# Attention and two feed-forward layers on one core: one block of the first product gathered in PSUM

## The chip, the cores and the metric

The kernel runs on one core of one Trainium2 chip. The metric is the device time of one execution in microseconds (us), from launch to the last store; lower is better. In the rows, PE is TensorE (the matmuls), PEld its weight loads, DVE is VectorE, ACT is ScalarE, POOL is GpSimd and SP is SyncE, which issues the transfers.

## The reference

An attention with local and strided masks is followed by two feed-forward layers on the same 2,304 tokens (model width 512, inner width 2,048), all in float32:

```python
x = attention(q, k, v)                  # 4 batches, 8 heads, 576 positions, width 64
h = x @ moe_w_in;   g = h * clip(h + 3, 0, 6) / 6
x = g @ moe_w_out
h = x @ moe2_w_in;  g = h * tanh(softplus(h))      # Mish
return g @ moe2_w_out
```

## The kernel before, in words

**Numbers and layout.** Activations lie transposed: `xs0` to `xs3` hold 128 of the 512 model columns each, with the tokens along the row. A matrix operand is split into a high and a low part, both of type fp32r, and a product is three matmuls (`mm3`, L1106 to L1108: low weights by high data, high by low, high by high). The weights of the input side are in tiles `win`, those of the output side in `wout`, the split data in `x` (5 slots) and `g`, `g_late` (9 slots).

**Two by two blocks in seven products.** Apart from the attention and a piece of the first layer (20 "plain" steps, until about 167 us), each feed-forward layer works on blocks: a unit is a range of 2 x 384 tokens and one or more slices `fp` of the inner width (names ending in 0 and 1 where a unit has two). In a unit the four blocks of the first product h (two halves of tokens by two halves of the slice, called a11, a12, a21, a22) come from seven block products in place of eight, after Winograd. Each of the seven is two `mm3` (q = 0, 1), so six matmuls of 128x384. `PRODUCTS` (L45) is the order of the seven, and `CHAIN` says which are added up in the same PSUM bank: bank a takes a11, s2, s1, s4 one after the other, bank b takes s3 and a22, bank c takes a12. There are 42 pairs of a unit and a slice that go this way, 18 in the first layer and 24 in the second.

**What happens between the products.** `first_evict` reads a bank when a product has been added to it, before the next product may add more. Three sums are snapped to SBUF tiles by a copy (`c` after a12, `v` after s3, `u` after s2); then DVE adds a later state of another bank onto the tile: c + a11 gives block a11, u + a22 gives a21, v + s1 gives a22. The fourth block stays in bank a until s4 has been added. `activated` then applies the activation: in the first layer a Relu6 on ACT and a product on DVE (L1238, L1240), in the second a Mish on ACT (L1247), which needs another table of functions than the attention and the first layer, so that one ACT_TABLE_LOAD stands ahead of the first Mish. The four activated blocks are summed and split into `g`, and a second set of seven products with `wout` adds up the layer's output in `xs`.

**Who sets the order.** No queue or scheduler of the compiler decides: `Plan` (L150 to L304) simulates the engines with costs, factors (`SLOW`), due times and small constants (`FIRST_PACE`, `SOON`, `OVERLAP`, `BIAS`, `GUARD_DVE`, ...), and emits the instructions of each engine in the order that comes out. Each engine takes its rows in that order. The plan also picks the PSUM bank: first products use banks 0 to 3, second products banks 4 to 7; an operation with `frees` gives a bank back. Operations without a fixed engine (`add(None, ...)`) go to whichever the plan finds done first. The plan knows nothing of the ACT_TABLE_LOAD. While PE works on the first products of one unit it also works on the second products of the unit before, in turns that the plan mixes.

In the attention (16 units of a batch and two heads, in among the plain steps) the sums of the softmax get a guard against zero (L735 on ACT or L737 on DVE; `GUARD_DVE` says for how many units DVE does it). POOL or DVE then multiplies the exponentials `e` (L741), which PE transposes (L750).

Of the kernel before, what the change touches and what calls it, by code (L numbers as in the profile page):

```python
# [41 lines left out]

BOTH = ((0, 0, 0), (0, 1, 1, 1))

PRODUCTS = ("a12", "a11", "s3", "s2", "a22", "s1", "s4")  # L45
SECOND = ("a11", "s3", "s2", "a22", "s1", "a12", "s4")
CHAIN = {"a11": "a", "s2": "a", "s1": "a", "s4": "a", "a12": "c", "s3": "b", "a22": "b"}
W_OF = {"a11": (0, 0), "a12": (0, 1), "s2": (2, 6), "s1": (2, 8), "s4": (1, 4), "s3": (3, 10), "a22": (3, 12)}
# [31 lines left out]


ORIGIN = 600
START, FIRST_PACE = 26026, 2749
UNIT = 113
MASKS_DUE = 18211

SOON = 57

HALF_ROWS = 1.8

SPLIT = 2
KEEP, SWITCH = 1413, 100
GUARD_DVE, AGAIN_POOL, ABS_DVE = 0, 4, 1
HALF_PACE = 4687
EARLY_W, EARLY_G, EARLY_X = 10496, 7917, 10732
OVERLAP = 15258
UNIT_Y, UNIT_X = 11126, 19146
LEAD = 0.1313


BIAS = {"act": -116, "dve": 455, "pool": 239}
FIRST_BIAS = {"act": -1424, "dve": 440, "pool": 9}
BIAS_FROM = 37262

SLOW = {"pe": 1.0, "act": 1.0405, "dve": 1.0525, "pool": 0.9269, "dma": 1.2861}

# [210 lines left out]
def copy_ns(n, psum=False):  # L319

    return {"act": act_ns(n, psum), "dve": dve_ns(n if psum else n / 2)}
# [17 lines left out]
def attention_then_two_ffns(ctx, tc, qkv, masks, wts, out):  # L339
# [20 lines left out]
    add = plan.add  # L360
# [9 lines left out]
    pool = ctx.enter_context(tc.tile_pool(name="main", bufs=1, side="right"))  # L370
# [70 lines left out]
    t = START  # L441
# [776 lines left out]
    def build(u):  # L1218
# [32 lines left out]
        def chain_of(keys, use, before, product, evict, first_due):  # L1251


            nonlocal due
            due = first_due
            banks_of = {(c, key): Bank(use) for c in "abc" for key in keys}
            last, gone = {}, {}
            for i, kind in enumerate(PRODUCTS if use == "h" else SECOND):
                c = CHAIN[kind]
                for key in keys:  # L1260
                    bank, started = banks_of[c, key], (c, key) in last
                    deps = [*last.get((c, key), []), *gone.get((c, key), [])]
                    if i == 0:
                        deps.extend(before)
                    prev = None
                    parts = product(i, kind, key)
                    for x, (more, emit) in enumerate(parts):
                        due += cost
                        prev = add(
                            "pe", cost, lambda emit=emit, bank=bank, first=not started and x == 0, last=x == len(parts) - 1: emit(banks[bank.n][:, :n], first, last),  # L1270
                            [prev, *deps, *more], due=due, bank=None if started or x else bank,
                        )
                        if not started and x == 0:
                            opened[use].append(prev)
                    last[c, key] = [prev]
                    gone[c, key] = evict(i, kind, key, prev, bank, lambda bank=bank: banks[bank.n][:, :n])

        x_now, snaps = {}, {}

        def first_product(i, kind, fp):  # L1280

# [17 lines left out]
        def first_evict(i, kind, fp, o, bank, psum):  # L1299

            x_now[kind][2].append(o)
            if u.closes:
                in_use[m, fp][W_OF[kind][0]].append(o)
            if kind in ("a12", "s3", "s2"):
                at = snaps[kind, fp] = take({"a12": "c", "s3": "v", "s2": "u"}[kind])
                o = add(None, copy_ns(n, True), lambda eng: copy(eng, at.tile(), psum()), [o, *at.old], frees=bank if kind == "a12" else None)
                at.ready = [o]
                return [o]
            if kind == "s4":
                activated(fp, "a12", psum, [o], take("t"), bank)  # L1310
                return []
            of, to = {"a11": ("a12", "a11"), "a22": ("s2", "a21"), "s1": ("s3", "a22")}[kind]
            at = snaps[of, fp]
            o = add(
                "dve", dve_ns(n), lambda: nc.vector.tensor_tensor(at.tile(), psum(), at.tile(), ALU.add),
# [236 lines left out]
```

## Time and profile before

| | before |
|---|---|
| runs, us | 821.84, 823.63, 823.14 (median 823.14) |
| the profiled execution's own time, us | 823.42 |
| its span, first to last instruction, us | 821.6 |
| mean granted TensorE clock | 0.996 |
| DVE busy, us (share) | 699.0 (85%) |
| ACT busy, us (share) | 440.9 (54%) |
| POOL busy, us (share) | 244.7 (30%) |

The page of a profile counts as busy the time in which an instruction of the engine runs; matmuls overlap, each 128x384 one is shown as 0.33 us long while the next starts 0.17 us after it. So for PE the distance between starts says more than the busy time. In the timeline "[0.36 <-PE bank L1108]" behind a row means that the engine stood idle for 0.36 us ahead of it and what ended that. "x2" is a run of like instructions drawn together. Rows name tiles without their numbers.

### The profile page before, as it was taken

To read this page: it belongs to the slowest core of one execution; us is meant where nothing else is said; L and a number is where in the kernel's file an instruction comes from. 1 tells how busy PE (TensorE), PEld (TensorE's weight loads), DVE (VectorE), ACT (ScalarE), POOL (GpSimd) and SP (SyncE) were. 2 spreads that over 40 slices of the span, in tenths; PEclk is the share of its full clock that TensorE was granted. 3 is DMA by queue.
4 is the path that set the end of the run, shared out by engine and by line. 5 is a ranking of instruction groups with operands and counts; after the bars stand their busy time and mean duration, and the time that the engine had idled before them with its cause. 6 is when DMAs were issued, how large, how long until landed. Compare 5 with 4: busy or idle time off the path is not lost.

```text
span 821.6 us, 17074 instructions
## 1 busy us (share of the span) xinstructions
PE 809.5 (99%) x6672; PEld 776.9 (95%) x6672; DVE 699.0 (85%) x1332; ACT 440.9 (54%) x936; POOL 244.7 (30%) x229
## 2 busy tenths in 40 slices
PE   8899999999999999999999999999999999999998
PEld 5678888899999999999999999999999999999998
DVE  5699977899999657997999999966999999998666
ACT  2576667676554434444446567545455554455442
POOL 3424321112322200111214223100556544564332
PEclk9899999999999999999999999999999999999999
DMA  7966671466678587865774545865767766765832
GB/s 224 245 190 212 208 224 40 167 249 254 247 284 321 192 291 235 270 247 201 265 254 187 226 165 240 280 215 190 262 226 243 242 214 234 251 213 189 256 116 106
DMA packets 49381, 182.32 MB, mean 222 GB/s; under 512 B 6292, under 2 KB 15636, under 8 KB 49300
## 3 DMA queue, kind: packets, MB, share of 16 engines
q1 hardware_dynamic: 49300, 181.23, 64.4%
q8 instruction: 52, 0.85, 0.4%
q14 instruction: 29, 0.24, 0.1%
HBM read 138.74 MB, written 42.47 MB: 221 GB/s over the span
## 4 chain that ended last, share of the span: by engine, by line
PE 95%; DMA 2%; SPq 1%; DVE 1%; issue 1%; ACT 0%; POOL 0%; ACTq 0%; POOLq 0%
PE bank L1106 30%; PE bank L1108 29%; PE bank L1107 29%; PE bank L796 2%; PE bank L644 2%; DMA xs<-in_qkv_dram 1%; PE bank L750 1%; SPq L533 1%; DMA y<-keep 0%; PE bank L752 0%; PE bank L701 0%; PE bank L1476 0%; ACT pt L365 0%; SPq L880 0%; DVE xs L1379 0%
## 5 line engine op out<-in xcount | busy, mean ns | idle before, releaser
L1106 PE MATMUL bank<-x,win 128*128 128x384 f32 (+3 forms) x668 | 228.1, 341 | 0.5 <-POOL win L857 0.5
L1107 PE MATMUL bank<-x,win 128*128 128x384 f32 (+3 forms) x668 | 226.2, 339 | 0.0
L1108 PE MATMUL bank<-x,win 128*128 128x384 f32 (+3 forms) x668 | 226.1, 338 | 0.0
L1106 PE MATMUL bank<-g,wout 128*128 128x384 f32 (+3 forms) x512 | 176.0, 344 | 0.2 <-DVE xs L1379 0.2
L1108 PE MATMUL bank<-g,wout 128*128 128x384 f32 (+3 forms) x512 | 174.0, 340 | 0.0
L1107 PE MATMUL bank<-g,wout 128*128 128x384 f32 (+3 forms) x512 | 173.9, 340 | 0.0
L1106 PEld LDWEIGHTS bank<-x,win 128*128 128x128 f32 x668 | 125.4, 188 | 4.2 <-POOL win L857 0.9
L1107 PEld LDWEIGHTS bank<-x,win 128*128 128x128 f32 x668 | 125.4, 188 | 2.4 <-DVE x L857 0.4
L1108 PEld LDWEIGHTS bank<-x,win 128*128 128x128 f32 x668 | 125.4, 188 | 2.2
L1389 DVE TENSOR_TENSOR xs<-bank,xs 128x384 f32<-128x384 f32 x174 | 95.3, 550 | 32.6 <-PE bank L1108 31.6
L1106 PEld LDWEIGHTS bank<-g,wout 128*128 128x128 f32 x512 | 96.1, 188 | 3.1 <-DVE xs L1379 0.8
L1108 PEld LDWEIGHTS bank<-g,wout 128*128 128x128 f32 x512 | 96.1, 188 | 2.3
L1107 PEld LDWEIGHTS bank<-g,wout 128*128 128x128 f32 x512 | 96.2, 188 | 1.7 <-issue 0.2
L1108 PE MATMUL bank<-g_late,wout 128*128 128x384 f32 x204 | 68.1, 334 | 0.0
L1106 PE MATMUL bank<-g_late,wout 128*128 128x384 f32 x204 | 68.1, 334 | 0.0
L1107 PE MATMUL bank<-g_late,wout 128*128 128x384 f32 x204 | 68.1, 334 | 0.0
L906 DVE SCALAR_TENSOR_TENSOR wa<-raw,wa 128x512 uint32<-128x512 uint32 x64 | 49.1, 769 | 0.4
L992 POOL TENSOR_TENSOR w<-w 128x256 f32<-128x256 f32 x21 | 17.7, 843 | 91.3 <-DVE w L923 87.4
L365 ACT CAST g<-t 128x384 fp32r<-128x384 f32 (+3 forms) x59 | 31.4, 536 | 19.9 <-DVE t L1167 6.8
L857 POOL TENSOR_TENSOR win<-w,win 128x512 fp32r<-128x512 f32 (+1 forms) x20 | 26.0, 1305 | 46.9 <-ACT win L365 35.0
L365 ACT CAST win<-w 128x512 fp32r<-128x512 f32 (+1 forms) x55 | 30.7, 570 | 16.4 <-DVE w L923 7.7
L365 ACT COPY v<-bank 128x384 f32<-128x384 f32 x42 | 20.1, 480 | 35.6 <-PE bank L1108 32.8
(151 smaller groups left out, 1469.5 us busy)
## 6 DMA issues: line engine op xcount, KB each, us to landing
x<-kept_s SPq DMA_DIRECT2D x60, 768.0 KB
x<-kept_a SPq DMA_DIRECT2D x45, 768.0 KB
raw<-in_wts_dram SPq DMA_DIRECT2D x64, 512.0 KB
kept_s<-x SPq DMA_DIRECT2D x24, 768.0 KB
kept_a<-x SPq DMA_DIRECT2D x18, 768.0 KB
qk<-in_qkv_dram SPq DMA_DIRECT2D x14, 576.0 KB
keep<-y SPq DMA_DIRECT2D x24, 192.0 KB
out_dram<-xs SPq DMA_DIRECT2D x24, 192.0 KB
```

Of the source, the lines that this page charges most:

```text
L365: nc.scalar.copy(out, src)
L533: return add("dma", 400, lambda: nc.sync.dma_start(to(rows), src), due=MASKS_DUE)
L644: nc.tensor.matmul(banks[both[h].n][g * QN:(g + 1) * QN, slot * WK:(slot + 1) * WK], src.q[h * D:(h + 1) * D, n // 6, n % 2 * QN:(n % 2 + ...
L750: nc.tensor.transpose(banks[turned[0].n][:, j * P:(j + 1) * P], e[:, t:t + 2].rearrange("p s k -> p (s k)"), ident)
L796: nc.tensor.matmul(o[h * D:(h + 1) * D], src.v[rows, NB + others(local).index(n) if n in others(local) else i, h * D:(h + 1) * D], pt[rows ...
L857: lambda eng: engines[eng].tensor_tensor(lo(), src(), hi().bitcast(F32), ALU.subtract),
L906: lambda: nc.vector.scalar_tensor_tensor(ai, high, 0xC0000000, ai, ALU.bitwise_and, ALU.bitwise_or),
L992: lambda eng: engines[eng].tensor_tensor(of[out], of[x], of[y], ALU.subtract), [*on[x], *on[y]], lock=("dve", "pool"),
L1106: nc.tensor.matmul(o, low_w, high, start=first, stop=False, skip_group_check=True)
L1107: nc.tensor.matmul(o, high_w, low, start=False, stop=False, skip_group_check=True)
L1108: nc.tensor.matmul(o, high_w, high, start=False, stop=last, skip_group_check=True)
L1389: "dve", dve_ns(n), lambda: nc.vector.tensor_tensor(y(), src(), y(), ALU.add), [prev, y_sums[key]], due=due, frees=frees,
```

## The change

a11 becomes the first product and a12 the second. When a11 is in bank a, it is copied from there into bank c (a copy from PSUM to PSUM) in place of a12's copy to the tile `c`. a12's matmuls then add onto that bank, so its first matmul no longer starts a new sum and has to come after the copy. The block a11 is complete in bank c after a12, the DVE add onto the tile `c` falls away, and the activation reads the bank and gives it back. s2 and s3 change places in the order of the products. The constants of the plan are new, all of them numbers that shift the order.

```diff
@@ -42,7 +42,7 @@
 
 BOTH = ((0, 0, 0), (0, 1, 1, 1))
 
-PRODUCTS = ("a12", "a11", "s3", "s2", "a22", "s1", "s4")
+PRODUCTS = ("a11", "a12", "s2", "s3", "a22", "s1", "s4")
 SECOND = ("a11", "s3", "s2", "a22", "s1", "a12", "s4")
 CHAIN = {"a11": "a", "s2": "a", "s1": "a", "s4": "a", "a12": "c", "s3": "b", "a22": "b"}
 W_OF = {"a11": (0, 0), "a12": (0, 1), "s2": (2, 6), "s1": (2, 8), "s4": (1, 4), "s3": (3, 10), "a22": (3, 12)}
@@ -80,29 +80,29 @@
 
 
 ORIGIN = 600
-START, FIRST_PACE = 26026, 2749
+START, FIRST_PACE = 26026, 2816
 UNIT = 113
 MASKS_DUE = 18211
 
-SOON = 57
+SOON = 63
 
 HALF_ROWS = 1.8
 
 SPLIT = 2
 KEEP, SWITCH = 1413, 100
-GUARD_DVE, AGAIN_POOL, ABS_DVE = 0, 4, 1
+GUARD_DVE, AGAIN_POOL, ABS_DVE = 2, 4, 1
 HALF_PACE = 4687
 EARLY_W, EARLY_G, EARLY_X = 10496, 7917, 10732
-OVERLAP = 15258
-UNIT_Y, UNIT_X = 11126, 19146
+OVERLAP = 20001
+UNIT_Y, UNIT_X = 11448, 19146
 LEAD = 0.1313
 
 
-BIAS = {"act": -116, "dve": 455, "pool": 239}
-FIRST_BIAS = {"act": -1424, "dve": 440, "pool": 9}
+BIAS = {"act": -55, "dve": 474, "pool": 239}
+FIRST_BIAS = {"act": -1424, "dve": 424, "pool": 9}
 BIAS_FROM = 37262
 
-SLOW = {"pe": 1.0, "act": 1.0405, "dve": 1.0525, "pool": 0.9269, "dma": 1.2861}
+SLOW = {"pe": 1.0, "act": 1.0417, "dve": 1.0525, "pool": 0.9235, "dma": 1.2861}
 
 
 
@@ -1255,11 +1255,16 @@
             due = first_due
             banks_of = {(c, key): Bank(use) for c in "abc" for key in keys}
             last, gone = {}, {}
+            if use == "h":
+                h_banks.update({key: banks_of["c", key] for key in keys})
             for i, kind in enumerate(PRODUCTS if use == "h" else SECOND):
                 c = CHAIN[kind]
                 for key in keys:
                     bank, started = banks_of[c, key], (c, key) in last
                     deps = [*last.get((c, key), []), *gone.get((c, key), [])]
+                    seeded = use == "h" and kind == "a12"
+                    if seeded:
+                        deps.extend(gone["a", key])
                     if i == 0:
                         deps.extend(before)
                     prev = None
@@ -1267,15 +1272,15 @@
                     for x, (more, emit) in enumerate(parts):
                         due += cost
                         prev = add(
-                            "pe", cost, lambda emit=emit, bank=bank, first=not started and x == 0, last=x == len(parts) - 1: emit(banks[bank.n][:, :n], first, last),
-                            [prev, *deps, *more], due=due, bank=None if started or x else bank,
+                            "pe", cost, lambda emit=emit, bank=bank, first=not started and not seeded and x == 0, last=x == len(parts) - 1: emit(banks[bank.n][:, :n], first, last),
+                            [prev, *deps, *more], due=due, bank=None if started or seeded or x else bank,
                         )
-                        if not started and x == 0:
+                        if not started and not seeded and x == 0:
                             opened[use].append(prev)
                     last[c, key] = [prev]
                     gone[c, key] = evict(i, kind, key, prev, bank, lambda bank=bank: banks[bank.n][:, :n])
 
-        x_now, snaps = {}, {}
+        x_now, snaps, h_banks = {}, {}, {}
 
         def first_product(i, kind, fp):
 
@@ -1301,15 +1306,20 @@
             x_now[kind][2].append(o)
             if u.closes:
                 in_use[m, fp][W_OF[kind][0]].append(o)
-            if kind in ("a12", "s3", "s2"):
-                at = snaps[kind, fp] = take({"a12": "c", "s3": "v", "s2": "u"}[kind])
-                o = add(None, copy_ns(n, True), lambda eng: copy(eng, at.tile(), psum()), [o, *at.old], frees=bank if kind == "a12" else None)
+            if kind == "a11":
+                to = h_banks[fp]
+                return [add(
+                    None, copy_ns(n, True), lambda eng: copy(eng, banks[to.n][:, :n], psum()), [o], bank=to,
+                )]
+            if kind in ("s3", "s2"):
+                at = snaps[kind, fp] = take({"s3": "v", "s2": "u"}[kind])
+                o = add(None, copy_ns(n, True), lambda eng: copy(eng, at.tile(), psum()), [o, *at.old])
                 at.ready = [o]
                 return [o]
-            if kind == "s4":
-                activated(fp, "a12", psum, [o], take("t"), bank)
+            if kind in ("s4", "a12"):
+                activated(fp, {"s4": "a12", "a12": "a11"}[kind], psum, [o], take({"s4": "t", "a12": "c"}[kind]), bank)
                 return []
-            of, to = {"a11": ("a12", "a11"), "a22": ("s2", "a21"), "s1": ("s3", "a22")}[kind]
+            of, to = {"a22": ("s2", "a21"), "s1": ("s3", "a22")}[kind]
             at = snaps[of, fp]
             o = add(
                 "dve", dve_ns(n), lambda: nc.vector.tensor_tensor(at.tile(), psum(), at.tile(), ALU.add),
```

How this moves rows shows best at three places. The first is ACT at the changeover from the first layer to the second; the names are those of the last section, x_73 is the split data, bank3_64 is PSUM bank 3. Before:

```order
L365 COPY v0_2317<-bank0_61 128x384
L365 CAST x_73<-f3_2312 128x384
L365 CAST x_73<-f0_2309 128x384
L365 CAST x_73<-f1_2310 128x384
L365 COPY c1_2314<-bank2_63 128x384
L1247 ACT_TABLE_LOAD
L1247 ACTIVATE c0_2313<-c0_2313 128x384
L1247 ACTIVATE c1_2314<-c1_2314 128x384
L365 COPY v1_2318<-bank2_63 128x384
```

The same place on ACT after the change:

```order
L365 COPY u0_2311<-bank2_63 128x384
L365 COPY v0_2313<-bank1_62 128x384
L1247 ACT_TABLE_LOAD
L1247 ACTIVATE c0_2309<-bank3_64 128x384
L365 COPY bank3_64<-bank0_61 128x384
L365 CAST x_73<-f2_2307 128x384
L1247 ACTIVATE c1_2310<-bank3_64 128x384
L365 COPY u1_2312<-bank0_61 128x384
```

The two slices of the unit now follow each other through bank 3: the Mish of c0 reads it and gives it back, and only then does the copy of the second slice's a11 go into it. The table load stands ahead of that Mish and behind the copy of v0.

On PE, at the same place after the change, the last matmul into bank 1 (which the copy of v0 reads) and the first one onto the copied bank 3 stand like this, with nine matmuls of the second products between them:

```order
L1108 MATMUL bank1_62<-x_73,win2_2302 128x384
L1106 MATMUL bank6_67<-g_74,wout0_71 128x384
L1107 MATMUL bank6_67<-g_74,wout0_71 128x384
L1108 MATMUL bank6_67<-g_74,wout0_71 128x384
L1106 MATMUL bank6_67<-g_74,wout0_71 128x384
L1107 MATMUL bank6_67<-g_74,wout0_71 128x384
L1108 MATMUL bank6_67<-g_74,wout0_71 128x384
L1106 MATMUL bank6_67<-g_74,wout1_72 128x384
L1107 MATMUL bank6_67<-g_74,wout1_72 128x384
L1108 MATMUL bank6_67<-g_74,wout1_72 128x384
L1106 MATMUL bank3_64<-x_73,win0_69 128x384
```

Before, the last matmul into bank 0 (which its copy of v0 reads) was followed by a longer run of wout matmuls; no matmul there waited for a Mish.

The second place is PE in one of the last units, where bank 1 gets the last matmul of a11 and bank 2, into which it is copied, gets the first matmul of a12, after the change:

```order
L1108 MATMUL bank1_62<-x_73,win2_2302 128x384
L1106 MATMUL bank3_64<-x_73,win0_69 128x384
L1107 MATMUL bank3_64<-x_73,win0_69 128x384
L1108 MATMUL bank3_64<-x_73,win0_69 128x384
L1106 MATMUL bank3_64<-x_73,win0_69 128x384
L1107 MATMUL bank3_64<-x_73,win0_69 128x384
L1108 MATMUL bank3_64<-x_73,win0_69 128x384
L1106 MATMUL bank2_63<-x_73,win2_2302 128x384
```

Six matmuls stand between the two; 31 of the 42 copied blocks have six, five have nine, three twelve, two fifteen and one 27. Before, no such pair exists, because a12's first matmul opened a bank of its own.

The third place is ACT in the first units of the attention, a piece of the difference:

```order
 L713 ACTIVATE e_147<-bank_63 128x320
 L713 ACTIVATE e_147<-bank_62 64x64
 L713 ACTIVATE e_147<-bank_62 128x256
-L735 ACTIVATE sum_155<-sum_155 128x5
-L735 ACTIVATE sum_155<-sum_155 128x4
 L887 ACTIVATE wa_82<-raw_80 128x512
 L713 ACTIVATE e_148<-bank_65 128x320
```

These two guards, and the two of the next unit, go to DVE (L737), behind the sums that they guard. PE's own order is the same before and after until about 137 us.

## Rows read from the trace of the kernel before

**Rows 1.** The page's head and busy times, us
```profile
span 821.6 us, 17074 instructions
...
PE 809.5 (99%) x6672; PEld 776.9 (95%) x6672; DVE 699.0 (85%) x1332; ACT 440.9 (54%) x936; POOL 244.7 (30%) x229
```

**Rows 2.** Windows: length, busy us of each engine, PEclk, DMA share, GB/s
```profile
23.69:30.52 6.83, 6.40 (x91) 5.58 (x91) 2.82 (x7) 2.74 (x9) 2.64 (x3) 0.50 1.06 224
49.00:65.00 16.00, 14.39 (x311) 11.17 (x296) 14.08 (x26) 11.11 (x21) 6.13 (x5) 1.00 0.67 202
137.00:230.00 93.00, 92.77 (x574) 86.83 (x573) 83.94 (x162) 61.28 (x133) 20.62 (x18) 1.00 0.58 216
230.00:818.00 588.00, 588.00 (x3392) 587.37 (x3390) 506.43 (x958) 294.71 (x620) 180.45 (x160) 1.00 0.65 228
```

**Rows 3.** Timeline of PE at 300 us: start, length, operation
```profile
299.68 0.33 PE L1107 MATMUL bank<-x,win 128*128 128x384 f32 x1
...
305.92 0.33 PE L1107 MATMUL bank<-g,wout 128*128 128x384 f32 x1
```

**Rows 4.** Waits of PE from 137 us on: total, times, longest
```profile
PE bank L1106 <- DVE xs L1379: 0.2, 1, 0.2
```

**Rows 5.** Groups by line and form: busy us, mean ns, idle before
```profile
L1315 DVE TENSOR_TENSOR c<-bank,c 128x384 f32<-128x384 f32 x42 | 22.9, 551 | 4.2 <-PE bank L1108 3.6 <-ACT c L365 0.3
...
L365 ACT COPY c<-bank 128x384 f32<-128x384 f32 x42 | 20.1, 479 | 31.7 <-PE bank L1108 31.3
...
L365 ACT CAST g<-f 128x384 fp32r<-128x384 f32 x36 | 18.5, 513 | 15.0 <-DVE f L1331 7.4 <-POOL f L1331 7.0 <-PE bank L1108 0.6
...
L1247 ACT ACTIVATE c<-c 128x384 f32<-128x384 f32 x24 | 12.4, 525 | 19.1 <-DVE c L1315 19.0
...
L1247 ACT ACTIVATE t<-bank 128x384 f32<-128x384 f32 x24 | 11.7, 490 | 4.2 <-PE bank L1108 4.0
```

**Rows 6.** Timeline at 223 us, an activation behind PE
```profile
223.14 0.34 PE L1108 MATMUL bank<-x,win 128*128 128x384 f32 x1
223.51 0.49 ACT L1238 ACTIVATE t<-bank 128x384 f32<-128x384 f32 x1 [0.71 <-PE bank L1108]
```

**Rows 7.** Timeline at 185 us, PE behind an add of DVE
```profile
185.48 0.54 DVE L1315 TENSOR_TENSOR u<-bank,u 128x384 f32<-128x384 f32 x1
...
186.08 0.19 PEld L1106 LDWEIGHTS bank<-x,win 128*128 128x128 f32 x1 [0.17 <-DVE u L1315]
186.18 0.34 PE L1106 MATMUL bank<-x,win 128*128 128x384 f32 x1
```

**Rows 8.** Timeline at 447 us, a copy between two uses
```profile
447.01 0.33 PE L1108 MATMUL bank<-x,win 128*128 128x384 f32 x1
...
447.44 0.48 ACT L365 COPY c<-bank 128x384 f32<-128x384 f32 x1 [0.36 <-PE bank L1108]
...
448.23 0.33 PE L1106 MATMUL bank<-x,win 128*128 128x384 f32 x1
```

**Rows 9.** Timeline of ACT at the changeover of layers
```profile
456.51 0.48 ACT L365 COPY c<-bank 128x384 f32<-128x384 f32 x1
457.01 1.28 ACT L1247 ACT_TABLE_LOAD   x1
458.30 0.94 ACT L1247 ACTIVATE c<-c 128x384 f32<-128x384 f32 x2
```

**Rows 10.** Timeline of the first unit's products e on POOL
```profile
14.32 1.29 POOL L741 TENSOR_TENSOR e<-e,sum 128x320 f32<-128x320 f32 x2 [2.63 <-DVE nmax L695]
...
16.86 0.36 PEld L750 LDWEIGHTS bank<-mk,e 128*128 128x128 f32 x2
```

**Rows 11.** Timeline of PE, its three long early waits
```profile
21.93 1.00 PE L644 MATMUL bank<-xs 64*32 64x64 f32 x71 [1.65 <-DMA xs<-in_qkv_dram]
24.12 0.43 PE L644 MATMUL bank<-xs 64*32 64x64 f32 x5 [1.18 <-issue]
...
50.84 0.43 PE L644 MATMUL bank<-qk 64*32 64x64 f32 x15 [1.61 <-issue]
```

## The prediction

> **What bounds the kernel now.** I read the page's head and busy times first, then the stretches, then PE's own rows, then its waits. TensorE (PE) is busy for 99% of the span [rows 1]. That share alone could hide loose pacing, so the stretches come next: from 230 us to 818 us PE is busy for 588.00 of 588.00 us at full clock, with 3,392 recorded matmuls, one per 588.00 / 3392 = 0.1733 us [rows 2]. Single rows give the same: from 299.68 to 305.92 us there are 36 starts of 128x384 matmuls in 6.24 us, 0.1733 us each [rows 3]. From 137 us to the end the view of waits shows one single wait of PE, 0.2 us [rows 4]. So in the two feed-forward layers PE runs from matmul to matmul; a busier or idler VectorE (DVE, 83.94 of 93.00 us in 137 to 230) matters only where it makes PE wait, and what can be won there is a few tenths of a microsecond.
>
> **What the change adds and removes.** PE has the same matmuls, line by line and shape by shape, and the copy of a block is an ACT operation before and after. So what changes on other engines pays or costs only through a wait of PE.
>
> *Work off DVE.* 42 adds c<-bank at 551 ns go, 22.9 us of DVE [rows 5]. The 42 ACT copies c<-bank at 479 ns are replaced by 42 copies from bank to bank. The 24 Mish of this block read PSUM: I take the 490 ns of t<-bank in place of the 525 ns of c<-c [rows 5]. All of this lies beside PE's 588 of 588 us; its worth is bounded by PE's waits for DVE in this part, 0.2 us [rows 4], and nothing below. I take 0. If a transfer or a decode behind DVE became late, that would be new, and nothing in the rows is near it.
>
> *The copy from bank to bank.* The trace has none. Nearest rows: PSUM to SBUF COPY 479 ns, SBUF to SBUF CAST 513 ns [rows 5]; I take 0.48, bounds 0.44 to 0.51 by the same distance on either side. The Trainium skill ("Perfetto Trace Analysis", section "Optimizing Scalar/DVE Operations") gives ScalarE about 93 ns of overhead on SBUF and 51 ns on PSUM, which agrees in sign with the 34 ns between these two rows and would put the copy at an estimated 0.44, the sums below 0.04 lower.
>
> *The new loop of PE through ACT.* The second part's first matmul must wait until the copy is done. Its parts have rows: from the start of the last matmul to the start of ACT, 223.51 - 223.14 = 0.37 us where ACT was free [rows 6]; the copy, 0.48; from the end of an evict to PE's matmul, 186.18 - (185.48 + 0.54) = 0.16 us, where the weight load shows DVE as its releaser [rows 7]. Sum 1.01 us. In 31 of the 42 places the new order has exactly six matmuls between (as in the second piece of PE's order above), so the first dependent matmul would start by itself 7 x 0.1733 = 1.21 us after the last one: 0.20 us to spare. The kernel before holds such a loop without a wait: matmul 447.01, copy 447.44, next matmul into that bank 448.23 [rows 8]. What a late ACT costs: if the copy finds a CAST of 0.51 us just begun, PE waits up to 0.51 - 0.20 = 0.31 us. All 31 late would be 31 x 0.31 = 9.6 us; none is 0. Which end? The old copy of the same block waited for PE for 31.3 of the 31.7 us that ACT was idle ahead of 42 such copies [rows 5], 0.75 us ahead of one on average: as a rule ACT stood ready. So I stay close to the lower end and take one late place, +0.3 us. The other 11 places have nine or more matmuls between and 0.7 us or more to spare: 0.
>
> *One place is not like the others.* At the changeover from the first layer to the second, ACT loads a table ahead of the first Mish. Before, it stands between the copy of c1 and the Mish of c0, both on SBUF, and no matmul needs that Mish soon: ACT loads from 457.01 for 1.28 us and goes on at 458.30 [rows 9], and PE has no hole there [rows 2]. After, the bank copy of the second block goes into bank3, which the Mish of c0 must first give back; that Mish has the load ahead of it, and the load has the copy of v0 ahead of it, which waits for the last matmul into bank1. PE has nine wout matmuls after that one, and then needs bank3. Chain from the start of that last matmul: 0.37 to ACT, 0.48 copy of v0, 0.02 gap, 1.28 load, 0.01, 0.49 Mish from PSUM, 0.03 gap, 0.48 bank copy, 0.16 to PE: 3.32 us. (The gaps of 0.02 and 0.01 are read in [rows 9], between one row's end and the next's start; the 0.03 is my estimate from them.) PE arrives after 10 x 0.1733 = 1.73 us. It waits 3.32 - 1.73 = **1.59 us**. Behind it on PE is everything, so it reaches the end in full. Bounds: 1.5 with the short copy, 2.1 if ACT is a CAST late at v0's copy.
>
> A rule of the skill bears on this one: "ScalarE: Activation LUTs", section "What ACT_TABLE_LOAD costs", has the load at about 1,283 ns and a drain of about 1,380 ns after it. The load agrees with the row (1.28), the drain does not show: the next ACTIVATE begins 0.01 us after the load. By the page the wait would be 2.97 us, by the row 1.59.
>
> *The first 137 us.* PE's order is the same there. Of the changed constants little reaches a wait: four guards of the softmax's sums (two took 0.53 us on ACT) go to DVE for the first two units. They sit ahead of POOL's products, 14.32 + 1.29 = 15.61, which PE's weight load wants at 16.86 [rows 10]: 1.25 us to spare against 0.53 us moved. I take 0, bounds -0.3 to +0.3. The long waits, 1.65 us for a transfer and 1.18 us for issue, and the half-rate stretch behind them (0.50 in 23.69 to 30.52 us, so 1.2 of 2.4 GHz; 6.83 / 2 = 3.4 us lost [rows 2, 11]) depend on early transfers whose issue order is unchanged for the first hundred; I take them as they are.
>
> *The end.* The last matmuls, DVE's add and the stores are the same rows in the same order: 0.
>
> Sum on the profiled execution: 823.42 + 1.59 + 0.3 = 825.3 us. It stands 0.28 above the median of the runs (823.14), so **825.0 us**, 1.9 us or 0.23% longer. What a measurement of this kernel can tell from no change is about 0.2%, 1.65 us: below 821.5 is faster, above 824.8 slower.
>
> **The rivals.**
> - *Not slower: the load is out of the way.* PE's wait at the changeover exists only if ACT begins the load after that last matmul. If ACT comes to the load early, or PE comes to bank3 1.6 us later for another reason, the loop is 2.03 us without the load against 1.73, a wait of 0.3 or none. Against it: ACT's order puts v0's copy ahead, and an engine takes its rows in order. For it: I read where PE and ACT meet from the order, not from a trace. With 0 to 0.3 there, the other late places at 0 to 0.3 and DVE's 0.2 back: 822.4 to 823.7. It decides once ACT is 1.6 us ahead.
> - *The loops are late in many places.* The removed DVE work and the new due times shift ACT's CASTs; if a third of the 31 places meets one, 10 x 0.31 = 3.1 us on top: 827.8. For it: 0.20 us to spare is less than any ACT row. Against it: the idle time before the old copies.
> - *A drain behind the load*: 1.38 us more, 826.4. Against it stands [rows 9].
> - *The wait at the changeover lowers the clock.* The early half-rate stretch followed waits of 1.65 and 1.18 us; a like stretch would cost 3.4 us: 828.4. Against it: the wait of 1.61 us at 50.84 was followed by a granted clock of 1.00 in 49 to 65 us [rows 2, 11].
> - *The early part gets better.* If moved guards or a moved subtraction let the first units' waits shrink so that the half-rate stretch is gone, 825.0 - 3.4 = 821.6. Against it: the first cause there is a transfer.
>
> **How the numbers follow.** Forecast 0.50, its own range 824.3 to 826.2 (0.32 of it above 824.8, 0.18 below). Not slower 0.24 (0.01 faster). Many loops late 0.12, drain 0.03, clock 0.03, all slower. Early part better 0.08 (0.05 faster). So faster 0.06, same 0.18 + 0.23 + 0.03 = 0.44, slower 0.32 + 0.12 + 0.03 + 0.03 = 0.50. The range runs from 822.2, which leaves out most of the early case and a little of the second, to 827.2, which leaves out the clock and about half of the many late loops: some 0.18 outside.
>
> **What the new profile would show.** Right: 42 ACT copies bank<-bank at about 0.48 us; no DVE c<-bank adds and DVE some 23 us less busy; one PE wait of about 1.6 us of an x,win matmul for ACT near the table load, with v0's copy just ahead of the load; the pace 0.1733 us elsewhere; the half-rate stretch where it was. Wrong: no such wait; or many short PE waits for the bank copies, 0.1 to 0.3 us each; or new waits on POOL's or DVE's splits, since the new constants move those too. What would upset it most is an ACT row ahead of the changeover that itself waits, for a slot of x whose store has not landed: each such microsecond adds to PE's wait one for one.

## The result

The changed kernel takes 827.58 us (median of 15 runs, 825.76 to 830.38), the kernel before 822.56 us beside it (15 runs, 820.15 to 826.36): ratio 1.006, 95% interval 1.0047 to 1.0074, some 5 us longer. The forecast was 825.0 us, 1.9 us longer, in a range from 822.2 to 827.2: the sign was right, and the loss is more than twice the forecast one.

The page of the profile after, head and busy times:

```profile
span 825.8 us, 17039 instructions
...
PE 809.8 (98%) x6672; PEld 776.1 (94%) x6672; DVE 690.9 (84%) x1317; ACT 434.4 (53%) x923; POOL 235.5 (29%) x215
```

Against [rows 1], DVE has 8.1 us less to do (699.0 to 690.9), ACT 6.5 and POOL 9.2 less, PE the same work. The forecast had 23 us less for DVE: the 42 adds are gone, but DVE's rows fell by 15 only (1332 to 1317), because the new plan gives it 27 others, 13 from ACT (936 to 923) and 14 from POOL (229 to 215). The span grew by 4.2 us all the same. What PE waits for from 137 us on, where [rows 4] had a single wait of 0.2 us:

```profile
PE bank L1106 <- ACT bank L365: 2.8, 4, 1.3
PE bank L1106 <- DVE win L857: 0.5, 1, 0.5
```

The windows of the same part (length, then the busy time of PE, PEld, DVE, ACT and POOL, the granted clock, DMA):

```profile
137.00:230.00 93.00, 92.42 (x569) 86.30 (x569) 87.62 (x169) 60.76 (x133) 22.64 (x18) 1.00 0.58 218
230.00:460.00 230.00, 228.16 (x1313) 227.28 (x1313) 185.87 (x355) 101.44 (x209) 55.03 (x48) 1.00 0.69 245
...
460.00:822.00 362.00, 360.98 (x2081) 360.34 (x2080) 308.60 (x577) 187.75 (x403) 114.70 (x99) 1.00 0.61 214
```

PE was busy for 588.00 of 588.00 us in [rows 2]; now 1.84 us are missing in the first long window and 1.02 in the second. The granted clock is 1.00 in all three, so it is waiting and not a slower clock. How the copy of the block changed (busy us, mean ns, idle time before):

```profile
L365 ACT COPY bank<-bank 128x384 f32<-128x384 f32 x42 | 19.3, 465 | 22.1 <-PE bank L1108 21.9
```

The 42 adds c<-bank of [rows 5] are gone, the 42 copies from bank to bank take 465 ns each.

**A measure that leaves the attention out.** The first part of the program starts with transfers and differs from run to run: the same changed kernel, profiled twice, reached its 2,951st matmul at 168.78 and at 171.33 us. From there to the start of the last matmul it took 653.33 and 653.39 us. So below, "layers" is the start of the last matmul less the start of the 2,951st, both read from the one profiled execution of each kernel (the changed one has two):

| kernel | 2,951st | last | layers, us | less before | ratio of run times, 95% interval |
|---|---|---|---|---|---|
| before | 169.51 | 817.93 | 648.42 | | |
| changed | 168.78 | 822.12 | 653.33 | +4.9 | 1.006 [1.0047, 1.0074] |
| changed, again | 171.33 | 824.73 | 653.39 | +5.0 | 1.0059 [1.0035, 1.0082] |
| load early | 165.39 | 818.39 | 652.99 | +4.6 | 1.0037 [1.0019, 1.0056] |
| copies first | 167.90 | 820.08 | 652.18 | +3.8 | 1.0039 [1.0017, 1.0061] |
| no loop | 169.30 | 820.78 | 651.49 | +3.1 | 1.0025 [1.0009, 1.0041] |
| both edits | 169.31 | 819.08 | 649.76 | +1.3 | 1.0031 [1.0009, 1.0054] |
| old constants | 167.71 | 823.40 | 655.68 | +7.3 | 1.0089 [1.0062, 1.0116] |
| old structure, new constants | 170.18 | 826.92 | 656.75 | +8.3 | 1.0090 [1.0060, 1.0120] |
| nine between | 168.37 | 819.88 | 651.51 | +3.1 | 1.0046 [1.0023, 1.0068] |
| all moved | 169.15 | 820.09 | 650.94 | +2.5 | 1.0041 [1.0025, 1.0057] |

The layers' 4.9 us are 0.6% of the run and, within the interval, the whole loss. Two things limit the column of layers. The 2,951st matmul does not part the work at quite the same place in every order (the number of matmuls with 320 in place of 384 columns behind it differs): 0.1 us between the kernel before and the changed one, up to 0.5 us for the old structure with new constants, by an estimate from the pace. And the repeat to 0.06 us was measured for the changed kernel alone. The intervals of the run times of the single edits overlap with that of the changed kernel run again, so what an edit gained is read from the holes in PE's starts and not from the run times.

The holes in PE's starts there, everything above the pace of 0.1733 us, add up: 1.51 us at 453, 0.27 at 199, 0.61 at 229, 0.64 at 604, 0.71 at 692, 0.66 at 264, 0.20 at 216, 0.09 at 354 (each named by the time at which it begins, or close to it), and about 0.11 more behind each of these eight, 5.6 us in all, against 0.8 us of such holes before.

**The changeover** is the place that the prediction computed. ACT and PE there, after:

```profile
451.74 0.33 PE L1108 MATMUL bank<-x,win 128*128 128x384 f32 x1
...
452.16 0.48 ACT L365 COPY v<-bank 128x384 f32<-128x384 f32 x1
...
452.65 1.28 ACT L1247 ACT_TABLE_LOAD   x1
...
453.30 0.34 PE L1108 MATMUL bank<-g,wout 128*128 128x384 f32 x1
453.95 0.49 ACT L1247 ACTIVATE c<-bank 128x384 f32<-128x384 f32 x1
...
454.47 0.46 ACT L365 COPY bank<-bank 128x384 f32<-128x384 f32 x1
...
454.99 0.45 PE L1106 MATMUL bank<-x,win 128*128 128x384 f32 x1 [1.35 <-ACT bank L365]
```

The copy of v0 follows the last matmul into its bank (451.74), then the load, the Mish, the bank copy, and PE at 454.99, 3.25 us after 451.74 (forecast 3.32). PE was ready 0.173 us after the start at 453.30, so the hole is 1.51 us (forecast 1.59). The next matmul behind it starts not 0.173 but 0.28 us later, in this and the other such places.

**A late copy**, as it looks at 604 us:

```profile
602.60 1.01 POOL L1341 TENSOR_TENSOR f<-f,c 128x384 f32<-128x384 f32 x1
...
603.15 0.33 PE L1108 MATMUL bank<-x,win 128*128 128x384 f32 x1
...
603.64 0.52 ACT L365 CAST g_late<-f 128x384 fp32r<-128x384 f32 x1 [1.11 <-POOL f L1341]
...
604.06 0.51 ACT L365 CAST g<-f 128x384 fp32r<-128x384 f32 x1
...
604.48 0.84 ACT L365 COPY bank<-bank 128x384 f32<-128x384 f32 x2
...
605.00 0.44 PE L1106 MATMUL bank<-x,win 128*128 128x384 f32 x1 [0.48 <-ACT bank L365]
```

The first slice's last a11 matmul starts at 603.15, so its copy could have begun by 603.52. But ACT stood at a CAST that waited for POOL's sum f until 603.64 (the bracket's 1.11 us), a second CAST followed, and the copy came at 604.48, 0.96 us late. The second copy (drawn together with the first, "x2") follows at once. PE had used up its time to spare and waited.

That time is more than the 0.20 us of the prediction. The first copy ends at 604.95 (mean length 465 ns) and PE starts at 605.00, 0.05 us behind it, where the prediction took 0.16 from [rows 7]. There PE was not waiting for DVE. The matmul ahead of that at 186.18 has 512 columns, and such matmuls start 0.23 us apart, so PE came no later than its own pace had it:

```profile
185.95 0.40 PE L1108 MATMUL bank<-g,wout 128*128 128x512 f32 x1
```

With 0.05, the loop takes 0.37 + 0.47 + 0.05 = 0.89 us and leaves 0.32 us. The holes follow from that: 0.96 us late less 0.32 is the 0.64 us at 604. At 692 the order on ACT is the same, two CASTs behind a sum of POOL, and the copy is 1.03 us late. At 229 it is 0.92 us late behind a single CAST, whose input t DVE finished only at 228.78. At 199 fifteen matmuls stand between the last one of a11 and the first one of a12, and the copy is still 2.1 us late, behind a run of ACT rows without a gap (CASTs of x and g, copies to keep). The copies of the other 37 blocks, late or not, cost PE nothing.

### The profile page after: what moved, and what is told of

It is laid out like the page before. It is cut to its first block, busy times and chain, and to the rows that moved or that the text cites. A ratio compares the mean times of both kernels' runs of the same rounds, so it can differ in the third digit from the quotient of the medians.

```text
span 825.8 us, 17039 instructions
## 1 busy us (share of the span) xinstructions
PE 809.8 (98%) x6672; PEld 776.1 (94%) x6672; DVE 690.9 (84%) x1317; ACT 434.4 (53%) x923; POOL 235.5 (29%) x215
## 4 chain that ended last, share of the span: by engine, by line
PE 86%; DVE 6%; ACT 2%; issue 2%; DMA 2%; POOL 1%; SPq 0%; ACTq 0%; DVEq 0%
PE bank L1106 27%; PE bank L1108 26%; PE bank L1107 26%; PE bank L796 2%; PE bank L644 2%; PE bank L627 1%; PE bank L750 1%; DMA v<-in_qkv_dram 1%; DVE g L857 1%; DVE xs L1399 1%; PE bank L701 1%; DMA raw<-in_wts_dram 1%; POOL f L1341 1%; POOL g L857 1%; DVE wa L897 1%
## 5 line engine op out<-in xcount | busy, mean ns | idle before, releaser
L906 DVE SCALAR_TENSOR_TENSOR wa<-raw,wa 128x512 uint32<-128x512 uint32 x64 | 45.6, 717 | 0.4
L1325 DVE TENSOR_TENSOR u<-bank,u 128x384 f32<-128x384 f32 x42 | 23.2, 552 | 22.7 <-PE bank L1108 22.3
```

Source lines behind the costliest of these rows:

```text
L906: lambda: nc.vector.scalar_tensor_tensor(ai, high, 0xC0000000, ai, ALU.bitwise_and, ALU.bitwise_or),
```

## The experiments

**The changed kernel once more**, beside the next three kernels and on the same chip.

> The changed kernel once more, as the reference of this group on the same chip. Both theories: span near 825.8 us, ratio to the kernel before 1.005 to 1.007, PE's waits from 137 us on for the bank copies about 2.8 us in four places.

Layers 653.39 us, the same holes at the same places to 0.04 us. The span was 828.4 us, not the expected 825.8: 2.6 us more than the first profile, nearly all of it ahead of the 2,951st matmul.

**The table load earlier.** One Mish of a single column, on a tile of its own, stands ahead of the first copy of u:

```diff
+                if m == 1 and kind == "s2" and not load_before:
+                    load_before.append(o)
...
+        nc.gpsimd.memset(gap[:, :2], 0.0)
         for op in plan.run():
+            if load_before and op is load_before[0]:
+                nc.scalar.activation(gap[:, :1], gap[:, 1:2], AF.Mish)
```

> The changed kernel with one Mish of a single column ahead of the first unit's copy of u0, where ACT was idle for 1.87 us, so that the table load runs there; everything else in the same order. Theory (PE waits for the bank copies on ACT): the wait at the changeover falls from 1.35 us to about 0.3 us (chain 2.0 us against 1.73 us), the span by 1.0 to 1.3 us, ratio to before about 1.0045. Rival (the loss is the new constants' doing, by transfers and splits that come late; the copies are only where PE happens to wait): a new wait opens behind it, span within 0.4 us of the changed kernel, ratio 1.006.

The load now lies in idle time of ACT:

```profile
447.46 1.28 ACT L1498 ACT_TABLE_LOAD   x1
...
450.20 0.50 ACT L1247 ACTIVATE c<-bank 128x384 f32<-128x384 f32 x1
450.73 0.46 ACT L365 COPY bank<-bank 128x384 f32<-128x384 f32 x1
```

The hole at the changeover went from 1.51 to 0.10 us, more than was expected (0.3). But the layers gained only 0.3 to 0.4 us, for at 233 us, more than 200 us ahead of the edit, a hole of 0.81 us had come up that the two runs of the changed kernel don't have, and PE's waits show it as one for DVE:

```profile
PE bank L1106 <- ACT bank L365: 1.5, 3, 0.5
PE bank L1106 <- DVE c L1240: 0.6, 1, 0.6
PE bank L1106 <- DVE win L857: 0.5, 1, 0.5
```

It is DVE's product c<-c,bank, which since the change is what gives bank c back. The trace shows why it came late: DVE had stood idle for 1.42 us ahead of an add whose second input, keep, comes by a transfer from DRAM.

```profile
228.79 0.56 DVE L1392 TENSOR_TENSOR xs<-bank,keep 128x384 f32<-128x384 f32 x1 [1.42 <-PE bank L1107]
```

The view names PE, but the last matmul into that bank had started at 223.15; the last piece of the transfer landed at 228.70, 4.7 us after its issue (223.96). From there DVE ran its rows one behind the other until the product ended at 234.16, and PE started at 234.22. In the changed kernel the same two transfers cost DVE 0.31 us in one profile and nothing in the other, and PE did not wait. So this hole comes from a late transfer that meets the held bank, and not from the edit; ahead of it the edit has but one row, the memset on POOL at the program's start. The theory is right on the changeover; without this hole (0.81 us and 0.11 behind it) the gain would have been some 1.3 us, by an estimate. Of the rival's new wait behind the changeover there is none.

**Six copies ahead of CASTs.** The plan is made as before, then six of the 42 copies are moved on ACT (number of the copy: places):

```diff
-        for op in plan.run():
+        for op in ahead(plan.run(), {2: 1, 4: 1, 28: 2, 29: 1, 34: 2, 35: 1}):
```

> The changed kernel with six of its 42 bank copies moved ahead of the one or two CASTs that stood before them in ACT's queue, at 199, 229, 605 and 693 us; all other engines in the same order. Theory (a bank copy queued behind a late CAST makes PE wait): the four late places, 0.3 + 0.6 + 0.6 + 0.7 us and 0.1 us of slow restart each, go, span 2.2 to 2.7 us shorter, ratio to before about 1.003. Rival (the CASTs are needed as much): the waits move to the splits behind the CASTs, span less than 0.8 us shorter, ratio 1.005 to 1.006.

The copy at 604 us is now ahead of both CASTs and PE goes on without a hole:

```profile
602.71 0.33 PE L1108 MATMUL bank<-x,win 128*128 128x384 f32 x1
...
603.14 0.46 ACT L365 COPY bank<-bank 128x384 f32<-128x384 f32 x1 [1.05 <-PE bank L1108]
...
603.51 0.52 ACT L365 CAST g_late<-f 128x384 fp32r<-128x384 f32 x1
...
603.92 0.33 PE L1106 MATMUL bank<-x,win 128*128 128x384 f32 x1
```

The holes at 229, 604 and 692 us are gone and that at 199 fell to 0.15, some 2.4 us with their slow restarts (the wait at 199 is too short for the view of waits, which counts four waits for a copy in the changed kernel; the starts show it). 1.15 us of the layers' time were gained; the rest went to DVE:

```profile
PE bank L1106 <- ACT bank L365: 1.3, 1, 1.3
PE bank L1106 <- DVE win L857: 0.6, 1, 0.6
PE bank L1106 <- DVE c L1240: 0.5, 1, 0.5
PE bank L1106 <- DVE v L1326: 0.4, 1, 0.4
```

The one for ACT is the changeover. Waits for c<-c,bank at 235 us (a hole of 0.68), for v at 215 (0.53) and for win at 264 (0.81) are new or longer. The first is the place of before, again behind a transfer:

```profile
229.97 1.14 DVE L1390 TENSOR_TENSOR xs<-bank,keep 128x384 f32<-128x384 f32 x2 [0.46 <-DMA keep<-y]
```

PE now comes there 0.7 us earlier, since it no longer waits at 229, and DVE does not. So the theory is right for the places that it named, not for the span (2.2 to 2.7 us were expected), and the rival is right that part of it comes back, though at other rows than the splits behind the CASTs.

**No loop at all.** The copy goes to a tile that nobody reads, and a12 starts a sum of its own; a11 is left out of the block:

```diff
-                    None, copy_ns(n, True), lambda eng: copy(eng, banks[to.n][:, :n], psum()), [o], bank=to,
+                    None, copy_ns(n, True), lambda eng: copy(eng, aside[:, :n], psum()), [o], bank=to,
...
-                            "pe", cost, lambda emit=emit, bank=bank, first=not started and not seeded and x == 0, last=x == len(parts) - 1: emit(banks[bank.n][:, :n], first, last),
+                            "pe", cost, lambda emit=emit, bank=bank, first=not started and x == 0, last=x == len(parts) - 1: emit(banks[bank.n][:, :n], first, last),
```

> The changed kernel, same order on every engine, with the 42 bank copies written to a tile in SBUF (bf16) that nobody reads, and a12's matmuls starting a new sum, so that no matmul waits for such a copy; it leaves a11 out of the block. Theory (the loop from PE through ACT to PE is the whole loss): all waits for bank copies go, 1.5 + 2.2 + 0.6 us, span 4.0 to 4.4 us shorter, ratio to before 1.000 to 1.001. Rival (constants and order): span within 1 us of the changed kernel, ratio 1.005 to 1.006.

```profile
PE bank L1107 <- DVE c L1241: 1.1, 1, 1.1
PE bank L1107 <- ACT c L1248: 0.9, 1, 0.9
PE bank L1107 <- DVE win L858: 0.5, 1, 0.5
PE bank L1107 <- DVE v L1326: 0.2, 1, 0.2
```

No wait for a copy is left, and 1.8 us of the 4.9 are gone; the theory had 4.0 to 4.4, the rival less than 1. Two of the remaining waits are for the bank itself: PE may not start a new sum in bank c before the block's last reader has been there. At the changeover that is the Mish behind the load (0.9 us), at 236 us DVE's product (1.1 us). Part of the second is again the late transfer:

```profile
231.53 1.13 DVE L1390 TENSOR_TENSOR xs<-bank,keep 128x384 f32<-128x384 f32 x2 [1.04 <-DMA keep<-y]
```

My theory of one loop was too narrow: the change adds a second dependence, since bank c is held until the activation has read it, where it was given back by a copy before.

**Both edits.** The early load and the six copies together.

> The changed kernel with both edits of before: the table load in ACT's earlier idle time, and the six bank copies ahead of the CASTs. Theory (both waits are separate and add up): from the 2951st matmul to the last 653.3 us less 1.4 less 2.0, about 650 us (kernel before: 648.4), ratio to before 1.002 to 1.003, what is left being waits for DVE at 215, 235 and 264 us. Rival (one stall covers another): 651.5 us or more.

```profile
PE bank L1106 <- DVE win L857: 0.5, 1, 0.5
PE bank L1106 <- DVE v L1328: 0.4, 1, 0.4
```

Layers 649.76 us, 3.6 us less than the changed kernel, as the theory had it. Singly the two edits had gained 0.3 and 1.15 us, so what adds up are the holes that they remove (1.4 and 2.4 us) and not the times: in both single runs the hole behind the transfer, 0.9 and 0.8 us, stood against them, and here it is 0.11 us. What is left are the two DVE waits, a hole of 0.67 us at 264 and one of 0.52 at 216, and small ones (0.14 at 200, 0.10 at the changeover).

**Which half loses, structure or constants?** The changed structure with the constants of before (eight lines such as `-OVERLAP = 20001` and `+OVERLAP = 15258`):

> The changed kernel's structure (block gathered in PSUM) with every constant of the plan as in the kernel before. Theory (the structure costs, whatever the constants): again waits of PE for bank copies and for banks that are given back late, 2 to 8 us more from the 2951st matmul on than the kernel before's 648.4 us, ratio 1.003 to 1.010. Rival (the new constants lose): within 1 us of 648.4, ratio 0.999 to 1.001.

And the structure of before with the constants of the changed kernel:

> The kernel before's structure (copy to SBUF, DVE add) with every constant of the plan as in the changed kernel. Theory: no loop, so few waits: 648 to 650 us from the 2951st matmul on, ratio 1.000 to 1.002. Rival (the new constants lose): 651 to 654 us, ratio 1.004 to 1.006.

Waits of PE in the first, then in the second:

```profile
PE bank L1106 <- ACT v L365: 2.2, 1, 2.2
PE bank L1106 <- ACT bank L365: 1.4, 1, 1.4
PE bank L1106 <- DVE t L1240: 1.2, 1, 1.2
```

```profile
PE bank L1106 <- DVE xs L1379: 3.1, 4, 0.9
PE bank L1106 <- DVE win L857: 2.6, 3, 1.2
PE bank L1106 <- ACT c L365: 0.8, 1, 0.8
```

Both are slower than the changed kernel, by 2.3 and 3.4 us of the layers. The first came out as its theory had it. That the old structure with new constants is the worst of all was foreseen by neither theory: it has no loop, a copy gives bank c back, and 8.3 us are lost, 5.7 us of it in waits for DVE and 0.8 for that copy. A set of constants gives an order that fits one structure; the old structure's 648.42 us is its own constants' as much as the structure's. So neither half by itself "is" the loss, and the changed kernel's 4.9 us is what this pair leaves.

**Nine matmuls between.** The plan is told of what it lacks, 0.52 us more behind a bank copy and 1.29 us for the first Mish:

```diff
-                    r = max(d.end + (0 if d.engine == u.engine == "pe" else self.AFTER[d.engine]) for d in u.deps)
+                    r = max(d.end + (0 if d.engine == u.engine == "pe" else self.AFTER[d.engine]) + d.more for d in u.deps)
...
+                seed_ops[-1].more = 520
...
-                o = add("act", act_ns(n, psum), lambda: nc.scalar.activation(at.tile(), src(), AF.Mish), [*deps, *old], frees=frees)
+                o = add("act", act_ns(n, psum) + (0 if mish else LOAD), lambda: nc.scalar.activation(at.tile(), src(), AF.Mish), [*deps, *old], frees=frees)
```

> The changed kernel, where the plan counts 0.52 us more between a bank copy and the matmuls onto it, and 1.29 us more for the first Mish; all 42 copied blocks then have nine matmuls or more between (before: 31 with six); the order of all engines is planned anew. Theory (0.2 us to spare is too little, 0.7 us is enough): hardly a wait for a bank copy is left, 648.5 to 651 us from the 2951st matmul on, ratio 1.000 to 1.004. Rival (banks held longer cost as much): waits for DVE's or ACT's last reading of a bank grow, 652 us or more.

```profile
PE bank L1108 <- DVE v L1330: 1.3, 1, 1.3
PE bank L1108 <- DVE u L1242: 0.2, 1, 0.2
PE bank L1108 <- ACT bank L367: 0.2, 1, 0.2
```

Waits for bank copies fell from 2.8 to 0.2 us, as the theory expected (by PE's starts, where the short ones show too, from 3.7 to 0.7 us of holes). Layers 651.51 us, between the theory's 651 and the rival's 652: the biggest wait left, 1.3 us for DVE's v at 707 us, is one that no kernel before it had. The order was planned anew, so this is not the held bank of the rival (that one is a hole of 0.18 us at 237) but again an order that has its own late row.

**All moved.** The kernel with both edits and five more rows moved by one place:

```diff
-        for op in ahead(plan.run(), {2: 1, 4: 1, 28: 2, 29: 1, 34: 2, 35: 1}):
+        for op in ahead(plan.run(), {2: 2, 3: 1, 4: 1, 28: 2, 29: 1, 34: 2, 35: 1}):
...
+        for i in (358, 433, 436):
+            q = queues["dve"]
+            q.insert(i - 1, q.pop(i))
```

> The kernel with both edits, and five more rows moved by one place on their engines: two bank copies near 199 us ahead of a copy and a CAST, DVE's add onto v at 216 us ahead of a product that runs 1.64 us, and at 264 us DVE's product w and its split of win each ahead of the row before it. Theory (gathering in PSUM costs nothing by itself, all of the loss is in rows that stand in the wrong order for it): from the 2951st matmul to the last 649.8 less 1.3 to 1.5, that is 648.2 to 648.6 us against 648.4 of the kernel before, ratio 0.999 to 1.002, and not faster, since PE has no more waits to lose. Rival (each row moved makes another late): 649.5 us or more, ratio 1.002 to 1.004.

Layers 650.94 us, longer than with both edits alone: holes of 0.34 at 216 and 0.31 at 265 are shorter, but new or larger ones of 0.26 at 204, 0.30 at 231, 0.25 at 237 and 0.79 at 354 stand beside them. The rival holds. That gathering in PSUM costs nothing once the rows stand right was not shown.

## Why the prediction was right and wrong

*What bounds the kernel, and the upside.* Right. DVE's 8.1 us less bought nothing, since PE had 0.8 us of holes to lose in the layers (the view of waits, which the prediction went by, shows 0.2 of it); no kernel here came below 648.42 us.

*The changeover.* Right, mechanism and size: 1.51 us against 1.59. That the size is so close has some luck in it: PE came 0.06 us behind the copy in place of 0.16, ACT began 0.42 us behind the matmul in place of 0.37. The load ran 1.28 us and the Mish began 0.02 us after it (452.65 + 1.28 = 453.93, 453.95), as [rows 9] had it. The drain of some 1,380 ns behind a load that the Trainium skill gives ("ScalarE: Activation LUTs", section "What ACT_TABLE_LOAD costs") shows in neither kernel, and that rival fell. The early load took 1.41 of the 1.51 us away. The clock stayed at 1.00 after the wait, so the rival of a lower clock fell too. What was missing is the slow restart: the first matmul behind a wait is 0.44 us long and its successor starts 0.28 us after it, 0.11 us more each time.

*The loop of PE through ACT.* This step failed. It read "I stay close to the lower end and take one late place, +0.3 us", and behind it stood the bound "up to 0.51 - 0.20 = 0.31 us" for a copy that finds one CAST just begun. Measured are four places of 42, at 0.27, 0.61, 0.64 and 0.71 us, with their restarts 2.65 us in place of 0.3. Three of them are among the 31 with six matmuls between, far fewer than the third of the rival. The fourth, at 199, is one of "the other 11 places", which stood at 0. The time to spare was taken too small (0.20; it is 0.32 us), but the lateness of a copy far too small: 0.92 to 1.03 us at the three and 2.1 at the fourth, in place of at most 0.51. A copy can stand behind two CASTs, the first of which itself waits for POOL (604 and 692), behind one that waits for DVE (229), or behind a whole run of ACT rows (199). The rival of many late loops named this mechanism; that its 827.8 us lies so near the measured 827.58 is luck, since it had ten places at 0.31. The idle time of the old copies in [rows 5] said that ACT stood ready on average; it didn't say what stands ahead of a copy in the new order in the places where it doesn't. The order shows that. The six moved copies bore it out.

*DVE at 0.* Failed. The adds that left did no harm, but the new order brought waits for DVE: 0.66 us at 264 (win), 0.20 at 216 (v), 0.09 at 354 (win) and their restarts, 1.3 us. The prediction named "new waits on POOL's or DVE's splits" only as a sign of being wrong, at no price. Two of these are DVE rows that were late because rows ahead of them ran beside POOL. At 264:

```profile
258.29 1.32 POOL L857 TENSOR_TENSOR g<-c,g 128x384 fp32r<-128x384 f32 x1 [3.38 <-ACT g L365]
...
258.66 1.36 DVE L857 TENSOR_TENSOR g<-t,g 128x384 fp32r<-128x384 f32 x1
...
259.57 1.33 POOL L857 TENSOR_TENSOR g<-t,g 128x384 fp32r<-128x384 f32 x1
...
259.95 1.24 DVE L897 TENSOR_SCALAR wa<-wa 128x512 f32<-128x512 f32 x1
...
264.71 0.68 DVE L857 TENSOR_TENSOR win<-w,win 128x512 fp32r<-128x512 f32 x1
...
265.44 0.44 PE L1106 MATMUL bank<-x,win 128*128 128x384 f32 x1 [0.50 <-DVE win L857]
```

Rows of these two kinds take 0.55 and 0.42 us where POOL is idle, so 1.6 us are lost to POOL here, and DVE ran without a gap from there to the split that PE waited for, 0.66 us too late. At 216 the product u<-f,u ahead of the add onto v took 1.45 us in place of 0.55, beside a split of win on POOL (213.66 to 215.13). No run moved a POOL row by itself, so this is read from the rows and not shown by an experiment. Outside the changeover the held bank makes no hole in the two profiles of the changed kernel; in five of the experiments it does, near 235 us (0.18 to 1.24 us).

*The first 137 us.* Taken as 0, and no steady change shows: against the one profile of before, the changed kernel was 0.7 us ahead at its 2,951st matmul in one profile and 1.8 behind in the other. The bounds of 0.3 us to either side were too narrow for what two runs of one kernel differ by here. The half-rate stretch did not stay where it was: from 23.69 to 30.52 us the granted clock was 0.50 before, and 0.75 and 1.00 in the two profiles of the changed kernel, the second of which had 0.81 from 31.5 to 49 us.

Sum of the layers after the fact: 1.62 for the changeover, 2.65 for the late copies, 1.3 for DVE, less the 0.8 of before and with the 0.1 by which the 2,951st matmul parts the two orders differently: 4.9 us. The first two are shown by edits that took 3.8 us of these holes away; the third is read from the rows.

Still open is whether an order exists that has none of these waits: I moved rows and others came late in their place. A plan tuned further with this structure might reach the 648 us of before; nothing here suggests that it could go under by more than the 0.8 us.

## What to carry to other kernels

Where PE has no holes, taking work off another engine can't pay, and each new dependence of PE on another engine's queue can only cost; price it by what stands ahead in that queue in the new order, with that row's own wait, not by the engine's average idle time. A latency is read best where the engine behind it really waited, not where its own pace held it. A plan that has no price for a table load can put it where a chain is tight, as here; a tiny early activation in idle time moves it. Constants of a scheduler belong to the structure that they were fitted to: either half of such a change alone was slower than both together, so a structure can't be judged by one run with borrowed constants.

## What the runs showed of the hardware

A PE that has waited takes about 0.11 us to get back to its pace: the first matmul lasts 0.44 in place of 0.33 us, the next one starts 0.28 in place of 0.17 us later, in all eight places. The rows of the weight loads suggest why: in the stream a matmul's weights begin to load one matmul ahead of it (at 604.02 for the one at 604.19), but behind a wait they begin with it (both at 605.00). PE starts 0.05 to 0.06 us after the end of the ACT or DVE row that it waited for, in all eight places too. An ACT copy of 128x384 from bank to bank takes 465 ns, from PSUM to SBUF 479, from SBUF to SBUF with a CAST 513 ([rows 5]). A DVE row can stand still beside a POOL row: among kinds of DVE rows with five or more instances, 87 in the changed kernel took over 0.3 us longer than the shortest of their kind, and all 87 overlapped a POOL row, as did all 83 before (most of the 416 and 444 that overlapped one were not stretched so far). The two transfers keep<-y ahead of the place at 235 us landed 2.3 to 4.7 us after their issue (2.3 and 2.5 in the changed kernel's second profile, 3.7 in its first, 4.4 and 4.5 without the loop). And the part with the attention and its transfers varies by some 2.5 us between two runs of one kernel, while the 653 us behind it repeated to 0.06 us in those two; the late transfer of the early load shows that they need not.
